# One batch's activations transposed by DMA instead of by TensorE, and a hand-written instruction order replaced

## The chip, the core and the metric

The kernel runs on one core of one Trainium2 chip. The metric is device time in microseconds (us) for one execution. Six engines matter: TensorE (PE in the profile; its weight loads, PEld, overlap the matmuls), VectorE (DVE), ScalarE (ACT), GpSimd (POOL), SyncE (SP, which issues DMAs), and the DMA engines, which are shared by all queues. In this kernel POOL issues all loads from DRAM except two, and SP issues the stores of the output and all DMA transposes. Each engine takes its instructions strictly in the order in which they were written; an instruction waits, on semaphores, for what it reads and for the buffers that it overwrites.

## What is computed

Causal attention with a window of 64 positions, followed by a two-layer network with the shrink function h - tanh(h):

```python
batch, n_heads, seq, head_dim = (8, 8, 576, 64)
n_tokens, d_model, d_ff = (4608, 512, 2048)

scores = scale * np.matmul(q, k.transpose(0, 1, 3, 2))
mask = (rel >= 0) & (rel < window)          # rel = query position - key position, window = 64
scores = np.where(mask, scores, -1000000000.0)
attn = softmax(scores)
attn_out = np.matmul(attn, v)
x = attn_out.transpose(0, 2, 1, 3).reshape(B * S, H * D)
h = x @ w_in
g = h - np.tanh(h)
return g @ w_out                            # 4608 x 512, float32
```

## The kernel before

**Attention.** A batch has 576 positions, that is nine windows of 64, and eight heads, taken as four pairs. Pair number g belongs to batch g // 4. For batches 0 to 2 q and k of a pair are loaded (steps `lk`, `lq`), cast to another layout (`ck`, `cq`), transposed by TensorE (`Fp` for k, `Ep` for q) and copied out of PSUM (`Fc`, `Ec`); `Rp` computes the scores of a pair in two groups, `Rx` the exponentials. From batch 3 on, q and k are loaded as token rows (`qr.b.i`, `lr.b.i`, five tiles of up to 128 tokens each) and transposed by DMA (`tq.b.i`, `tk.b.i`, on SP); `tz.b` copies the last 64 columns of q, `S.g` computes the scores of two pairs at once and `Sx` the exponentials. `M.g` masks (DVE). `PP.g` multiplies the probabilities of two pairs with v, with the sums in an extra column; `DR` and `DN` (DVE) divide and write x into the tile `xs`, two buffers, by batch modulo 2. v is loaded by `LV.b.i` (or `lv`, `lt` for batch 1) into `vw`, two buffers; since a window of keys straddles two row tiles, a copy across the partition halves follows: `Z.b` on DVE (lines 151 and 152), or `za`, `zb` for batch 1.

**The two layers.** The 4608 tokens are nine chunks of 512. x must stand with features on partitions. This is done for batches 0 to 3 by TensorE: `Xp.b.half.part.bank` transposes four or five windows (line 397) into a PSUM bank and `Xc` copies them into `xT`, the chunk tile. For batches 4 to 7 `Y.b.half` does it by DMA from `xs` on SP: a batch's nine windows lie in two chunks, so each `Y` issues two transposes. `H.c.m` is the first layer of chunk c for 128 of the 2048 hidden features (four matmuls of 512 columns, line 431); `Hp.c.m.half` is one half of it (line 508, two matmuls, those that need features half 0 or half 1 alone). `A` is tanh (ACT, line 439), `G` subtracts it (DVE, line 445). `W.c.s.part` is the second layer for 128 tokens and a quarter of the hidden features (four matmuls, line 474), and `O.c.s.engine` copies the finished PSUM bank to SBUF and issues its store from SP.

**The order.** The Tile framework runs with a manual schedule: no scheduler moves anything. A string, `PLAN`, lists some 1170 steps, and `play` calls them one after another; each appends its instructions to the queues of its engines. The order of the words in `PLAN` is thus the order of every engine's queue. A word's last letter, where there is one, names the engine: p POOL, a ACT, v DVE, s SP. PSUM has eight banks; two or three take turns for `H`, one or two for `W`, and the numbers in `Rp`, `Fp`, `Ep`, `Xp` name the others.

The steps that the diff and the prediction touch:

```python
    def x_dma(b, half):
        lo, hi = b * NJ, (b + 1) * NJ
        while lo < hi:
            c = lo // WPC
            to = min(hi, (c + 1) * WPC)
            nc.sync.dma_start(out=chunk_tile(c)[:, lo - c * WPC:to - c * WPC, half],
                              in_=xs[b % 2][:, half, lo - b * NJ:to - b * NJ].rearrange("p w r d -> p (w r d)"),
                              transpose=True)
            lo = to
```

Of the kernel before, what the change touches and what calls it, by code (L numbers as in the profile page):

```python
# [15 lines left out]
def kernel(  # L16
# [515 lines left out]
    def play(script):  # L532
# [21 lines left out]
        Rx.7.1.3 cq.9.v H.0.14 M.4 wo.3 zb.1.3.p G.0.12 Ec.8.1.a PP.4 wo.1 A.0.14 H.0.15 mk DR.4 DN.4.1 G.0.14  # L554
        A.0.15 H.0.13 DN.4.0 za.1.3.a W.0.0.0 Rp.8.0.3 G.0.15 A.0.13 Rp.8.1.5 DN.4.2 zb.1.2.a za.1.2.v Rx.8.1.5
        W.0.1.0 M.7 qr.3.3 LV.2.3 lk.11.p PP.6 Rx.8.0.3 Xp.1.0.1.3 W.0.0.2 G.0.13 Xp.1.0.0.4 DR.6 Xc.1.0.1.3.a
        DN.6.2 DN.6.0 W.0.1.2 DN.6.1 Xp.1.1.0.5 lk.10.p ck.9.a Xc.1.0.0.4.a Fp.9.3 Xc.1.1.0.5.a Xp.1.1.1.4
        lr.3.2 lq.10.p lq.11.p LV.2.2 Hp.1.0.0 Ep.9.7 Xc.1.1.1.4.v Ec.9.7.a Fc.9.3.a Hp.1.0.1 W.0.1.3 W.0.0.3
        qr.3.4 LV.2.0 Rp.9.1.5 Rp.9.0.3 LV.2.1 W.0.0.1 O.0.0.a M.8 LV.2.4 W.0.1.1 lr.3.1 lr.3.4 A.1.0 tq.3.4
        G.1.0 O.0.1.a Rx.9.1.5 Rx.9.0.3 ck.11.a M.9 ck.10.a W.0.2.1 W.0.2.0 W.0.2.3 W.0.2.2 W.0.3.2 qr.3.1  # L560
        O.0.2.a Fp.11.5 cq.10.v W.0.3.1 W.0.3.3 Hp.1.1.1 W.0.3.0 Fp.10.7 Ep.10.3 Hp.1.1.0 O.0.3.v Ec.10.3.v
        Hp.1.2.1 Hp.1.2.0 Fc.10.7.a A.1.1 A.1.2 Rp.10.1.3 G.1.1 cq.11.v G.1.2 Fc.11.5.a H.1.3 Ep.11.6 tk.3.2
        A.1.3 Rx.10.1.3 H.1.4 A.1.4 G.1.3 Ec.11.6.a H.1.5 A.1.5 qr.3.0 Z.2 H.1.6 qr.3.2 PP.8 G.1.5 Rp.11.0.3
        A.1.6 tk.3.1 tq.3.3 lr.3.0 H.1.8 Rx.11.0.3 G.1.4 G.1.6 DR.8 H.1.7 DN.8.2 A.1.8 A.1.7 H.1.9 tq.3.1 G.1.8
        H.1.11 G.1.7 A.1.9 tk.3.4 H.1.10 lr.3.3 A.1.11 A.1.10 DN.8.1 G.1.9 Rp.11.1.3 Rx.11.1.3 Rp.10.0.6 tq.3.2
# [12 lines left out]
        W.1.3.0 H.2.15 DN.14.2 O.1.3.a DN.14.1 A.2.15 A.2.14 DN.14.0 Xp.3.1.0.6 W.2.0.1 Xp.3.1.1.7 W.2.0.0
        G.2.14 W.2.0.2 Xc.3.1.1.7.v Xc.3.0.0.4.a Xc.3.1.0.6.a G.2.15 qr.5.0 Hp.3.0.0 W.2.0.3 Hp.3.1.1 Hp.3.1.0
        O.2.0.a A.3.1 W.2.1.1 Hp.3.0.1 W.2.1.2 G.3.1 tz.4.v A.3.0 S.16 Sx.16.2 W.2.1.3 Sx.16.1 G.3.0 H.3.3  # L580
        W.2.1.0 M.17 Sx.16.0 M.16 H.3.2 A.3.3 PP.16 G.3.3 O.2.1.a A.3.2 tk.5.2 qr.5.1 qr.6.4 H.3.5 LV.5.3
        W.2.2.1 DR.16 A.3.5 tk.5.1 DN.16.2 tq.5.2 G.3.2 DN.16.1 H.3.4 DN.16.0 Y.4.0 A.3.4 S.18 G.3.5 W.2.2.0
        H.3.7 G.3.4 Sx.18.1 A.3.7 Sx.18.2 G.3.7 W.2.2.3 H.3.6 A.3.6 Sx.18.0 tk.6.4 tk.5.3 tq.5.0 tq.5.1 H.3.9
        tk.5.0 M.19 W.2.2.2 G.3.6 qr.7.1 H.3.8 M.18 A.3.9 PP.18 A.3.8 O.2.2.v G.3.9 DR.18 G.3.8 DN.18.2 DN.18.1
        DN.18.0 W.2.3.0 W.2.3.3 H.3.11 qr.6.2 lr.6.0 LV.5.4 lr.6.2 LV.5.0 A.3.11 W.2.3.1 G.3.11 Y.4.1 tq.6.4
        H.3.10 W.2.3.2 A.3.10 tq.6.2 G.3.10 O.2.3.a H.3.13 H.3.14 A.3.13 LV.5.1 LV.5.2 lr.6.1 qr.6.1 A.3.14
        G.3.13 W.3.0.2 H.3.15 tz.5.v G.3.14 qr.6.3 H.3.12 W.3.0.0 A.3.15 G.3.15 Hp.4.1.0 A.3.12 G.3.12 Hp.4.1.1
        A.4.1 W.3.0.1 G.4.1 W.3.0.3 Hp.4.0.1 H.4.3 Hp.4.0.0 O.3.0.v tk.6.3 tk.6.2 A.4.0 S.20 A.4.3 Sx.20.2
        Sx.20.0 Sx.20.1 tq.6.0 tk.6.0 W.3.1.1 G.4.0 G.4.3 W.3.1.0 H.4.2 W.3.1.3 A.4.2 S.22 G.4.2 H.4.4 W.3.1.2
# [61 lines left out]
```

## Time and profile before

| | |
|---|---|
| runs | 307.33, 307.46, 308.23 us; median 307.46 |
| profiled execution | span 305.2 us, from the first to the last instruction |
| granted TensorE clock | full speed (1.00) in every 20 us stretch but the last (0.98) |
| TensorE busy | 297.8 us |
| DVE, ACT, POOL busy | 176.2, 157.5, 103.7 us |
| DMA | 36.77 MB in 132,878 packets, 119,920 of them under 512 bytes |

A row of the page's groups names line, engine, operation and tiles (out<-in), the number of instructions, then busy time and mean duration, then how long the engine was idle just before them and what ended that. A row of the timeline has start, duration of a merged group, engine and line, and in brackets the idle time before it with what ended it. The matmul pipeline overlaps: a matmul of 512 columns shows 380 ns, and starts every 216 ns behind another. Some matmul records are missing (2599 matmuls for 2632 weight loads), which leaves false idles of a fraction of a microsecond.

### The profile page before, as it was taken

What the parts mean: (1) busy time and instruction counts of PE and PEld (TensorE: products, weight loads), DVE (VectorE), ACT (ScalarE), POOL (GpSimd) and SP (SyncE); (2) the same over time, 40 slices, a digit from 0 to 9 for tenths busy, and PEclk for the clock granted to TensorE, in tenths of its full rate; (3) what the DMA queues carried; (4) which work ended last, traced back from release to release, by engine and by line L of the source; (5) the groups of instructions that cost most, each with busy time, mean ns of one, the idle gap of its engine ahead of it and who ended that gap; (6) DMA issues with size and microseconds to landing.
All of it is one profiled execution on the core that took longest, in us unless ns stands there. A gap on an engine that the chain in (4) does not pass through costs nothing.

```text
span 305.2 us, 6469 instructions
## 1 busy us (share of the span) xinstructions
PE 297.8 (98%) x2599; PEld 149.4 (49%) x2632; DVE 176.2 (58%) x316; ACT 157.5 (52%) x265; POOL 103.7 (34%) x141
## 2 busy tenths in 40 slices
PE   8999999999999999999999999999999999999995
PEld 3574555545455545444544444444544444444443
DVE  1687993289577745675387475657673645355300
ACT  1898975487565346534564645345633433433211
POOL 8989775800994290019005770000000000000000
PEclk9999999999999999999999999999999999999999
DMA  9999999995999999949999999560143010001112
GB/s 155 159 195 193 195 207 180 159 205 102 102 143 127 173 125 181 182 108 131 164 177 127 135 173 142 95 143 35 37 76 74 0 69 37 34 34 37 52 51 104
DMA packets 132878, 36.77 MB, mean 120 GB/s; under 512 B 119920, under 2 KB 127344, under 8 KB 132848
## 3 DMA queue, kind: packets, MB, share of 16 engines
q0 software_dynamic: 92752, 18.06, 85.3%
q1 hardware_dynamic: 40096, 18.30, 31.5%
q8 instruction: 20, 0.33, 0.5%
q14 instruction: 10, 0.08, 0.1%
HBM read 36.70 MB, written 9.44 MB: 151 GB/s over the span
## 4 chain that ended last, share of the span: by engine, by line
PE 87%; DVE 5%; ACT 3%; issue 2%; POOL 2%; DVEq 0%; ACTq 0%; POOLq 0%
PE ps L474 38%; PE ps L431 30%; PE ps L508 6%; PE ps L348 3%; PE ps L304 2%; DVE gT L445 2%; PE ps L397 1%; ACT th L439 1%; PE ps L286 1%; PE ps L467 1%; DVE pt L323 1%; PE ps L260 1%; PE ps L281 1%; PE ps L227 1%; POOL qall L110 1%
## 5 line engine op out<-in xcount | busy, mean ns | idle before, releaser
L445 DVE TENSOR_TENSOR gT<-ps,th 128x512 bf16<-128x512 f32 x144 | 97.2, 687 | 85.3 <-ACT th L439 84.6
L474 PE MATMUL ps<-w_out_sb,gT 128*128 128x512 bf16 x527 | 131.5, 380 | 2.2 <-issue 0.8
L439 ACT ACTIVATE th<-ps 128x512 f32<-128x512 f32 x144 | 84.7, 599 | 93.0 <-PE ps L431 79.7
L431 PE MATMUL ps<-xT,wi 128*128 128x512 bf16 x496 | 120.7, 380 | 0.1
L474 PEld LDWEIGHTS <-gT 128*128 128x128 bf16 x560 | 53.3, 98 | 61.4
L431 PEld LDWEIGHTS <-wi 128*128 128x128 bf16 x496 | 47.0, 98 | 54.3
L145 POOL DMA_DIRECT2D vw<-in_v_dram x35 | 30.0, 872 | 36.1 <-PE ps L348 33.5
L90 ACT ACTIVATE ysb<-ps 128x512 f32<-128x512 f32 (+1 forms) x24 | 14.2, 593 | 30.9 <-PE ps L474 30.2
L166 POOL DMA_DIRECT2D qall<-in_q_dram x25 | 21.7, 881 | 24.1 <-DMA qw<-qall 21.4
L166 POOL DMA_DIRECT2D kall<-in_k_dram x25 | 21.7, 875 | 10.4 <-DMA kw<-kall 4.8
L314 ACT ACTIVATE pt<-ps 128x1024 bf16<-128x1024 f32 (+1 forms) x30 | 23.3, 816 | 3.5 <-PE ps L304 3.2
L323 DVE TENSOR_TENSOR pt<-pt,ps 128x1152 bf16<-128x1152 bf16 x28 | 20.5, 749 | 5.1 <-ACT pt L314 3.2
L508 PE MATMUL ps<-xT,wi 128*128 128x512 bf16 x80 | 20.8, 380 | 0.0
L92 DVE COPY ysb<-ps 128x512 f32<-128x512 f32 (+1 forms) x11 | 7.1, 650 | 20.5 <-PE ps L467 13.2
L368 DVE TENSOR_TENSOR xs<-ps,rcp 128x384 bf16<-128x384 f32 x28 | 15.2, 550 | 0.3
L318 ACT ACTIVATE pt<-ps 128x640 bf16<-128x640 f32 (+1 forms) x24 | 14.7, 659 | 0.8 <-PE ps L286 0.8
L348 PEld LDWEIGHTS <-pt 128*64 128x64 bf16 x504 | 9.4, 112 | 6.3 <-DVE pt L323 2.1
L90 ACT ACTIVATE kt<-ps 128x576 bf16<-128x576 bf16 x10 | 6.5, 647 | 10.8 <-PE ps L256 6.8
L227 PE MATMUL ps<-warm 128*128 128x512 bf16 (+1 forms) x35 | 10.6, 435 | 1.1 <-DVE warm L207 1.1
L508 PEld LDWEIGHTS <-wi 128*128 128x128 bf16 x80 | 7.4, 98 | 8.5 <-issue 0.4
L348 PE MATMUL ps<-vw,pt 128*64 128x65 bf16 x504 | 11.0, 197 | 0.3 <-DVE pt L323 0.2
L365 DVE TENSOR_TENSOR xs<-ps,rcp 128x384 bf16<-128x384 f32 x14 | 7.7, 550 | 0.1
(74 smaller groups left out, 166.7 us busy)
## 6 DMA issues: line engine op xcount, KB each, us to landing
out_dram<-ysb SPq DMA_DIRECT2D x33, 256.0 KB, 3.1
vw<-in_v_dram POOLq DMA_DIRECT2D x28, 128.0 KB, 6.6
qall<-in_q_dram POOLq DMA_DIRECT2D x20, 128.0 KB, 7.5
kall<-in_k_dram POOLq DMA_DIRECT2D x20, 128.0 KB, 6.8
w_out_sb<-in_moe_w_out_dram POOLq DMA_DIRECT2D x4, 512.0 KB, 8.2
kall<-in_k_dram POOLq DMA_DIRECT2D x11, 144.0 KB, 6.3
qall<-in_q_dram POOLq DMA_DIRECT2D x11, 144.0 KB, 6.6
wi<-in_moe_w_in_dram POOLq DMA_DIRECT2D x3, 512.0 KB, 7.9
```

Source lines behind the costliest of these rows:

```text
L90: nc.scalar.activation(o, i, ACT.Copy)
L145: nc.gpsimd.dma_start(out=w[:, 2 * i + 1, :, 0:D] if i < NF else w[64:128, 2 * i, :, 0:D], in_=v[b, :, 128 * i:128 * i + n].rearrange("h p ...
L166: nc.gpsimd.dma_start(out=token_rows(b, n)[0:c, i], in_=(q if n == "q" else k)[b, :, 128 * i:128 * i + c].rearrange("h p d -> p h d"))
L314: nc.scalar.activation(o, sp, ACT.Exp, scale=scale)
L323: nc.vector.tensor_tensor(p, p, mask.unsqueeze(1).to_broadcast([128, 2 * NJ, 64]), ALU.mult)
L348: nc.tensor.matmul(ps[r, bank, 65 * i:65 * i + 65], PT[(g + r2) % NPT][:, j, r], vw[b % 2][:, j, p0 + r2 + NP * h, :], start=True, stop=True)
L368: nc.vector.tensor_tensor(xs[b % 2][:, p0 // 2, 0:6, n // 2, :], ov[:, :, 0:D], sums[g][:, n].to_broadcast([128, 6, D]), ALU.mult)
L431: nc.tensor.matmul(hp, w_in_tile(ki, m), chunk_tile(c)[:, n.start // 64:n.stop // 64, ki % 2, 64 * (ki // 2):64 * (ki // 2) + 64], start=( ...
L439: nc.scalar.activation(th[:, n], hp, ACT.Tanh)
L445: nc.vector.tensor_tensor(gT[c][:, m, columns(s)], hp, th, ALU.subtract)
L474: nc.tensor.matmul(yp, gT[c][:, m, s * 128:(s + 1) * 128], w_out_sb[:, m, :], start=n == 1 and i == 0, stop=n == 4 and i == 3)
L508: nc.tensor.matmul(hp, w_in_tile(half + 2 * i, m), chunk_tile(c)[:, :, half, 64 * i:64 * i + 64], start=n == 1 and i == 0, stop=n == 2 and ...
```

## The change

Only `PLAN` is changed; no function is. The first 230 words are the same in both, up to the masking step `M.4` in the last quarter of chunk 0's first layer. Behind it:

- `Xp.3.*` and `Xc.3.*` (18 transposes and four copies) are gone; `Y.3.0` and `Y.3.1` are new, each with two DMA transposes on SP.
- The casts of pairs 10 and 11 (`ck.10`, `ck.11`, `cq.10`, `cq.11`) go from ACT and DVE to POOL. Of batch 1's copies across halves `zb.1.3` goes from POOL to ACT, `za.1.3` from ACT to DVE and `zb.1.2` from ACT to DVE. `tz.4` goes from DVE to POOL, `tz.5` from DVE to ACT, and some twenty of the copies out of PSUM (`O`, `Xc`, `Fc`, `Ec`) change between ACT and DVE.
- Some of the banks of `Rp`, `Ep`, `Fp`, `Xp` of batches 1 and 2 are others.
- All other steps are the same ones in another order: loads, transposes on SP, both layers and the attention steps. `PP.24`, for instance, has 14 layer blocks' worth and a score block between the start of `PP.22` and itself (21 and one before), and the loads `LV.6.2`, `LV.6.0` and `lr.7.1` stand ahead of the loads that wait for `PP.22`.

```diff
-        Rx.7.1.3 cq.9.v H.0.14 M.4 wo.3 zb.1.3.p G.0.12 Ec.8.1.a PP.4 wo.1 A.0.14 H.0.15 mk DR.4 DN.4.1 G.0.14
-        A.0.15 H.0.13 DN.4.0 za.1.3.a W.0.0.0 Rp.8.0.3 G.0.15 A.0.13 Rp.8.1.5 DN.4.2 zb.1.2.a za.1.2.v Rx.8.1.5
...
-        Xp.3.0.1.3 A.2.8 G.2.8 tq.5.3 H.2.11 O.1.2.v PP.14 DR.14 H.2.10 A.2.11 A.2.10 Xc.3.0.1.3.v G.2.10
-        Xp.3.0.0.4 W.1.3.2 G.2.11 tq.5.4 W.1.3.3 H.2.12 A.2.12 H.2.13 Z.4 A.2.13 W.1.3.1 G.2.12 G.2.13 H.2.14
-        W.1.3.0 H.2.15 DN.14.2 O.1.3.a DN.14.1 A.2.15 A.2.14 DN.14.0 Xp.3.1.0.6 W.2.0.1 Xp.3.1.1.7 W.2.0.0
-        G.2.14 W.2.0.2 Xc.3.1.1.7.v Xc.3.0.0.4.a Xc.3.1.0.6.a G.2.15 qr.5.0 Hp.3.0.0 W.2.0.3 Hp.3.1.1 Hp.3.1.0
...
+        Rx.7.1.3 cq.9.v H.0.14 M.4 PP.4 wo.1 Ec.8.1.a G.0.12 Rp.8.1.3 A.0.14 wo.3 DR.4 DN.4.2 DN.4.0 G.0.14
+        DN.4.1 M.7 H.0.15 H.0.13 Ep.9.5 A.0.15 Rx.8.1.3 G.0.15 W.0.0.0 Xp.1.0.0.3 Rp.8.0.4 Xp.1.0.1.6 W.0.1.0
+        lk.10.p lk.11.p LV.2.0 lq.11.p LV.2.2 qr.3.1 lq.10.p lr.3.4 ck.11.p ck.10.p LV.2.3 cq.11.p LV.2.4 lr.3.3
+        lr.3.1 LV.2.1 lr.3.2 cq.10.p zb.1.3.a zb.1.2.v mk za.1.3.v Ec.9.5.a Rx.8.0.4 M.8 Xc.1.0.1.6.v za.1.2.v
...
+        W.0.2.0 W.0.2.3 W.0.3.1 Fc.9.3.a Rp.9.1.6 Rp.9.0.3 Rx.9.1.6 Rx.9.0.3 W.0.2.1 W.0.2.2 Ep.11.7 W.0.3.0
+        Fp.11.6 Fp.10.5 W.0.3.3 O.0.2.v M.9 G.1.0 Hp.1.1.1 Hp.1.1.0 Ec.11.7.a A.1.1 W.0.3.2 Fc.10.5.v G.1.1
+        Ep.10.5 H.1.3 Fc.11.6.a O.0.3.a A.1.3 Hp.1.2.1 Hp.1.2.0 Ec.10.5.a A.1.2 G.1.3 G.1.2 H.1.10 H.1.6
...
+        H.2.11 W.1.3.2 W.1.3.3 H.2.12 A.2.11 A.2.12 M.14 M.15 G.2.11 G.2.12 tk.4.0 tk.4.2 PP.14 W.1.3.0 H.2.14
+        W.1.3.1 A.2.14 DR.14 DN.14.0 DN.14.1 DN.14.2 LV.4.4 tz.4.p lr.6.2 G.2.14 H.2.13 Y.3.0 Y.3.1 qr.5.3
...
+        qr.6.4 qr.6.3 H.2.10 A.2.13 A.2.10 O.1.3.v G.2.13 W.2.0.1 H.2.15 G.2.10 S.16 W.2.0.0 A.2.15 G.2.15
+        Sx.16.0 Sx.16.2 M.16 Z.4 Sx.16.1 Hp.3.0.0 W.2.0.2 W.2.0.3 Hp.3.0.1 M.17 Hp.3.1.0 Hp.3.1.1 PP.16 A.3.0
...
+        W.3.3.0 H.4.12 H.4.11 tz.6.a A.4.12 G.4.12 W.3.3.2 H.4.10 A.4.11 A.4.10 G.4.11 G.4.10 W.3.3.3 H.4.13
+        S.24 LV.6.2 LV.6.0 lr.7.1 Y.5.0 Y.5.1 LV.7.4 LV.6.4 LV.6.3 lr.7.4 LV.6.1 qr.7.3 qr.7.0 LV.7.1 LV.7.2
+        qr.7.2 LV.7.0 tq.7.3 tq.7.1 tq.7.4 tq.7.0 lr.7.2 tk.7.1 tk.7.2 tq.7.2 O.3.3.v A.4.13 H.4.14 Sx.24.2
+        A.4.14 W.4.0.2 W.4.0.1 G.4.13 G.4.14 W.4.0.3 Hp.5.1.1 W.4.0.0 Sx.24.0 Sx.24.1 Z.6 M.24 M.25 Hp.5.1.0
+        A.5.1 O.4.0.a Hp.5.0.0 Hp.5.0.1 A.5.0 PP.24 W.4.1.0 W.4.1.2 G.5.1 DR.24 DN.24.1 DN.24.2 G.5.0 H.5.5
...
+        W.8.1.2 G.8.15 W.8.3.3 W.8.2.0 W.8.2.2 W.8.2.1 W.8.2.3 O.8.2.v W.8.3.2 W.8.1.3 O.9.0.v W.8.0.1 W.8.0.3
+        W.8.1.1 W.8.0.0 W.8.0.2 O.8.1.v O.8.0.a W.8.3.1 W.8.3.0 O.8.3.v"""
```

109 lines of the change are left out of this document (48 added, 61 removed).

## The prediction, made before the changed kernel was run

> **What bounds the kernel now.** I read the page's engine shares and chain first, then the windows view over the stretch that the diff touches (from block PP.4 to the last matmul), then the timelines of the engines around it. The page, and the one row of the windows view (length of the stretch, then busy time of PE, PEld, DVE, ACT, POOL):
>
> ```profile
> span 305.2 us, 6469 instructions
> PE 297.8 (98%) x2599; PEld 149.4 (49%) x2632; DVE 176.2 (58%) x316; ACT 157.5 (52%) x265; POOL 103.7 (34%) x141
> PE 87%; DVE 5%; ACT 3%; issue 2%; POOL 2%; DVEq 0%; ACTq 0%; POOLq 0%
> 38.69:301.90 263.21, 260.64 (x2105) 128.99 (x2138) 150.17 (x254) 128.28 (x217) 71.20 (x86) 1.00 1.14 112
> ```
>
> TensorE is the bound. In the 263.21 us concerned it is idle for 2.57 us, and part of that is only apparent: the page counts 2599 matmuls for 2632 weight loads, so 33 records are missing. Reordering alone can therefore win less than 2.57 us. What can win is less TensorE work; what can lose is any wait, because TensorE takes its blocks in the order of the list and nothing behind a late block overtakes it. DVE (150 of 263) and ACT (128) are a little over half busy.
>
> **The transposes taken out.** TensorE's timeline (start, duration of the merged group, instructions) has the four blocks of x of batch 3 among blocks of the two layers:
>
> ```profile
> 98.92 0.44 PE L397 MATMUL ps<-ident,xs 128*128 128x128 bf16 x5
> 99.20 1.03 PE L431 MATMUL ps<-xT,wi 128*128 128x512 bf16 x4
> ...
> 101.73 0.39 PE L397 MATMUL ps<-ident,xs 128*128 128x128 bf16 x4
> 101.95 1.89 PE L474 MATMUL ps<-w_out_sb,gT 128*128 128x512 bf16 x7
> ...
> 108.00 1.03 PE L431 MATMUL ps<-xT,wi 128*128 128x512 bf16 x4
> 108.86 0.39 PE L397 MATMUL ps<-ident,xs 128*128 128x128 bf16 x4
> 109.08 1.03 PE L474 MATMUL ps<-w_out_sb,gT 128*128 128x512 bf16 x4
> 109.95 0.44 PE L397 MATMUL ps<-ident,xs 128*128 128x128 bf16 x5
> 110.23 1.89 PE L474 MATMUL ps<-w_out_sb,gT 128*128 128x512 bf16 x7
> ```
>
> Matmuls overlap, so a block costs the distance to the next start, not its duration: 0.28 + 0.22 + 0.22 + 0.28 = **1.00 us** for 18 transposes. A layer block (H or W, four matmuls) costs 108.86 - 108.00 = 0.86. All other TensorE work is the same in both lists, block by block, and score, probability-value and full-array blocks change places 57 times in each, so the order adds no matmul time. The four PSUM copies that go with the transposes were on DVE and ACT, under TensorE's work: nothing.
>
> **Work moved between engines.** Four casts (two k, two q pairs of batch 2) go to POOL, three cross copies of v and about half of the output copies change between POOL, ACT and DVE. The copies lie under TensorE's blocks and have at least one block (0.86) of cover where a bank is reused, in both lists; if such a cover were short by 0.1 to 0.3 us it would cost that. Before's own wait of this kind, on TensorE's timeline:
>
> ```profile
> 90.14 0.47 PE L348 MATMUL ps<-vw,pt 128*64 128x65 bf16 x18
> 90.81 0.47 PE L348 MATMUL ps<-vw,pt 128*64 128x65 bf16 x18 [0.19 <-DVE pt L323]
> ```
>
> Such slips exist in the old list and will in the new; I let them cancel, with -0.5 (those of before vanish) to +0.5 as bounds.
>
> The casts stand in POOL's queue between loads, and each waits for its own load. No POOL cast of this shape (96x768) is in the trace. POOL's copy of v (view of tile vw, ns min/median/max) and its slowest row per element (groups by form, mean 293 ns), then the first and the last row of POOL's loads of that stage, and the time from issue to landing of its q load at 46.05:
>
> ```profile
> L92 POOL COPY vw<-vw x4: 612/614/642, 29.4 to 40.0; 64x520 bf16<-64x520 bf16 x4
> L231 POOL TENSOR_SCALAR_AFFINE_SELECT hide<-hide 128x128 bf16<-128x128 bf16 x1 | 0.3, 293 | 0.1
> 40.55 0.70 POOL L198 DMA_DIRECT2D w_out_sb<-in_moe_w_out_dram x1
> 58.73 1.80 POOL L166 DMA_DIRECT2D kall<-in_k_dram  x2 [0.34 <-issue]
> DMA to landing us min/median/max: 8.9/8.9/8.9
> ```
>
> By the copy's rate a cast is 614 x 768/520 = 0.9 us; by the slowest row it is 768 x 293/128 = 1.76. I take 0.9, since a cast is a copy. From 41.25 to 60.53 POOL issued 19 loads, 1.01 each with its waits. In the new list 14 loads and four casts stand before the last cast, cq.10: 41.25 + 14.1 + 3.6 = 59.0. Its user is Ep.10.5: from PP.4 (38.69) on stand 20 layer blocks' worth (17.2), two probability-value blocks (1.8), four score blocks, the transposes of x and five of q and k (about 3, at the rates of S below and of L397 above), so it is due near 60.7. 1.7 us of cover: **nothing**, with 0 and, at 1.76 a cast, 62.4, that is +1.7, as bounds. The loads of lq.11 and lq.10 are the fourth and seventh there; 8.9 us after an issue near 45 to 48 is before their casts.
>
> **x of batch 3 by DMA.** Two issues for each of Y.3.0 and Y.3.1, on SP, which waits most of the time. The time to landing depends on the loads beside them. Y.5.1's two issues (ns min/median/max, first and last start), the landing in us (min/median/max) of Y.4.1, of Y.5.0 and of Y.5.1, the loads that POOL begins 2 us ahead of Y.5.1, and on TensorE block PP.22, its next one, and a score block S:
>
> ```profile
> L416 SPq DMA_TRANSPOSE xT<-xs x2: 1180/1238/1295, 165.5 to 166.8; - x2
> DMA to landing us min/median/max: 4.9/6.0/7.1
> DMA to landing us min/median/max: 2.3/2.5/2.7
> DMA to landing us min/median/max: 7.6/7.9/8.2
> 163.41 4.18 POOL L145 DMA_DIRECT2D vw<-in_v_dram  x5 [18.06 <-PE ps L348]
> 162.51 0.77 PE L348 MATMUL ps<-vw,pt 128*64 128x65 bf16 x36
> 163.43 0.81 PE L474 MATMUL ps<-w_out_sb,gT 128*128 128x512 bf16 x3 [0.16 <-issue]
> ...
> 168.55 0.69 PE L304 MATMUL ps<-qw,kw 64*128 64x64 bf16 x34
> ```
>
> Without loads 2.5 us, with a burst that began 2 us ahead 7.6 to 8.2. Y.5.1's first issue, at 165.5, comes 3.0 us after its PP.22 starts at 162.51; Y.3.1 follows PP.14 in the same way. Its first half-chunk is used by Hp.3.0.1, behind PP.14 (0.92, from 162.51 to 163.43), a score block S (0.69 and its first two matmuls, 0.8) and 10.5 layer blocks: 0.92 + 0.8 + 9.0 = 10.7 us. POOL begins a burst there too, when tk.4.2 has landed. 3.0 + 4.9 to 3.0 + 7.6 is 7.9 to 10.6: just covered, so **nothing**; by the slowest row, 8.2, it is 0.5 late.
>
> **v of batch 6.** The tightest place I find is PP.24. It stands 14 layer blocks, a score block and PP.22 itself behind the start of PP.22: 12.0 + 0.8 + 0.92 = 13.7 us. Before PP.24, DVE must run Z.6 (the copies across partition halves, once LV.6.* has landed), M.24 and M.25. The masking M by the page's groups, Z alone on DVE, then Z beside POOL's loads; the landing of before's vw load at 165.8 and of the six vw loads from 163.4 on; and a stop of POOL in that burst:
>
> ```profile
> L323 DVE TENSOR_TENSOR pt<-pt,ps 128x1152 bf16<-128x1152 bf16 x28 | 20.5, 749 | 5.1 <-ACT pt L314 3.2
> 64.66 0.70 DVE L151 COPY vw<-vw 64x2080 bf16<-64x2080 bf16 x1
> 65.36 0.70 DVE L152 COPY vw<-vw 64x2080 bf16<-64x2080 bf16 x1
> ...
> 179.67 1.03 DVE L151 COPY vw<-vw 64x2080 bf16<-64x2080 bf16 x1
> 180.71 0.81 DVE L152 COPY vw<-vw 64x2080 bf16<-64x2080 bf16 x1
> DMA to landing us min/median/max: 8.1/8.1/8.1
> DMA to landing us min/median/max: 3.6/6.8/8.7
> 174.22 0.88 POOL L166 DMA_DIRECT2D qall<-in_q_dram  x1 [1.38 <-DMA xT<-xs]
> ```
>
> Z takes 1.4 to 1.85, and POOL is loading then, so 1.85. With M.24 (0.7) and the part of M.25 that the second half of PP.24 needs (0.35), LV.6.1 must have landed 13.7 - 2.9 = 10.8 us after PP.22's start. POOL's burst again begins 0.9 behind it, since LV.7.4 waits for PP.22, and LV.6.1 is fifth, behind three loads of 64 KB and one of 128, 448 KB with its own. The first landing row above is the one load that closed as many bytes in before's burst: issued at 165.8, landed at 173.9, 10.5 after the burst began. That gives 11.4: **0.5 us late** (0.6, less what DVE's pipelining takes off). Bounds: 0 if it lands by 10.8; the longest of that burst, 8.7 from an issue at +3.9, gives 12.6, 1.8 late. Behind Z.6, DVE's subtractions of chunk 5 wait too, but TensorE is then already standing at PP.24.
>
> On such copies beside POOL's loads the Trainium skill ("SBUF — State Buffer", Who interferes with whom) says that DVE copies in a two-port mode and POOL share one port pair as an exclusive lock, the loser waiting for the whole instruction. The four rows of Z agree that a copy suffers beside POOL (1.03 and 0.81 for 0.70). By that rule at its worst, a 0.9 us issue ahead of each copy, Z.6 takes 3.2 and the sum ends 1.35 us higher; the rows show a quarter of that.
>
> **The end.** The last output changes its mates: a store of 256 KB (O.8.0) is issued some 0.6 us before the last, of 64 KB. To landing, at the end:
>
> ```profile
> out_dram<-ysb SPq DMA_DIRECT2D x1, 192.0 KB, 1.9
> out_dram<-ysb SPq DMA_DIRECT2D x1, 64.0 KB, 1.6
> 301.60 1.03 SPq L485 DMA_DIRECT2D out_dram<-ysb  x2
> ```
>
> Before, 192 KB went 0.7 ahead of it. A quarter more bytes: **+0.1**, 0 to 0.4.
>
> **Sum.** The profiled execution spans 305.2, the runs' median is 307.46, 2.2 lie around the span in both. 307.46 - 1.00 + 0.5 + 0.1 = **307.06**, taken as 307.0. Its own range: 306.3 to 307.8.
>
> **Rivals.** *All in time.* LV.6.1 lands by 10.8 us and part of before's slips goes: 306.56 - 0.4 = 306.2. For it: the landing need be only 0.6 earlier, and three of the five loads are half size. Against it: Y.5.1 still runs through that burst. *x late.* Y.3.1 takes its 8.2 and its issue slips by one 1.2 us slot behind Y.3.0: Hp.3.0.1 stands 0.5 + 0.2 to 1.7, say 0.9, and with the 0.5 at PP.24 the time is 307.9. For it: a burst begins at the same moment. Against it: Y.4.1 had 4.9. *v later still (slower than before).* POOL can be stopped inside the burst until earlier DMAs are done, as by the 1.38 in the row at 174.22. If that falls ahead of LV.6.1 and it takes 8.7, it lands 3.9 + 1.4 + 8.7 = 14.0 us after PP.22, 3.2 late: 306.56 + 3.2 = 309.8; with half that stop, 309.1. It decides from a landing 12.7 us after PP.22, where the time passes 308.4. Against it: before's first stop in that burst came after eleven loads, not four. *Slow casts (slower).* At 1.76 each, and with lk.11 landing 8.9 us after an issue near 43, the first cast starts at 52; four casts (7.0) and the six loads between them (6.1) end at 65.1, 4.4 behind Ep.10.5's need: 311.5. Against it: the copy row.
>
> **How the numbers follow.** This kernel's measurement can tell about 0.3% (0.9 us) from no change: faster is below 306.54, slower above 308.38. Chances: forecast 0.42, all in time 0.28, x late 0.10, v later 0.14, slow casts 0.06. The first rival and a sixth of the forecast's range are faster: 0.35. The slower rivals with a few hundredths of forecast and x late: 0.25. The rest, 0.40, cannot be told from before. The range of 8 in 10 is 305.9 to 309.4: below, the first rival with 0.3 to spare; above, most of v later.
>
> **What would show it.** Right: L397 falls from 72 to 54, TensorE's busy time by 1.0 us or so, Hp.3.0.1 without an idle ahead of it, and at PP.24 an idle of about half a microsecond behind DVE's L151/L152 and a v load. Wrong: idle before the L508 block of chunk 3 behind a DMA into xT (x late), before L260 of pairs 10 or 11 behind a POOL copy (casts), or more than 1.9 us at PP.24. If TensorE's idle in the stretch behind PP.4 is 2 us above before's, some place that I gave full cover has none.

## The result

The changed kernel took 309.24 us (median of 20 runs, 307.31 to 312.88) against 307.77 for the kernel before (20 runs on the same chip, 307.02 to 309.03). The ratio is 1.0048, with a 95% interval of 1.0026 to 1.0069: **slower by 0.48%, some 1.5 us**, where a gain of 0.40 us, too small to tell from none, was forecast. The changed kernel's runs are also spread over 5.6 us, those of before over 2.0. Medians here and below are of all runs, while the ratios leave out single slow runs, over 1.5% above the fastest of their kernel (here the one at 312.88).

The profiled execution of the changed kernel took 308.1 us, less than the median. Its page (span, shares of the chain by engine, then two groups; the columns of a group are busy time and mean, then the idle time before and what ended it):

```profile
span 306.4 us, 6466 instructions
...
PE 59%; DMA 22%; POOL 10%; issue 4%; DVE 2%; SPq 1%; ACT 1%; POOLq 0%; DVEq 0%; ACTq 0%
...
L474 PE MATMUL ps<-w_out_sb,gT 128*128 128x512 bf16 x560 | 135.0, 379 | 1.4 <-ACT ysb L90 1.3
...
L166 POOL DMA_DIRECT2D qall<-in_q_dram x25 | 21.7, 878 | 23.0 <-DMA qw<-qall 22.2
```

Before, the chain that ended last was TensorE for 87%, and DMA did not appear in it at all. Now DMA has 22% of it and POOL 10%. And TensorE's second layer has an idle of 1.3 us that was ended by a copy on ACT into `ysb`, the buffer for the output. POOL's loads of q were held 22.2 us by a DMA transpose; this is not new, since the page of the kernel before has 21.4 us for it.

The stretch from block PP.4 to the last matmul (window, its length, then busy times of PE, PEld, DVE, ACT, POOL), to be read against the 263.21 of before:

```profile
39.25:303.19 263.94, 262.16 (x2121) 128.27 (x2120) 151.35 (x255) 122.04 (x206) 74.28 (x90) 1.00 1.17 114
```

It is 0.73 longer, although 1.00 of TensorE work is gone. TensorE's busy time says nothing here: 33 matmul records were missing before, and now the page counts 2614 matmuls for 2614 weight loads.

**Where it stands.** The changed kernel's TensorE timeline has one idle of more than half a microsecond behind PP.4, at W.3.3.1, the block ahead of PP.22:

```profile
163.66 1.02 PE L474 MATMUL ps<-w_out_sb,gT 128*128 128x512 bf16 x4 [1.34 <-ACT ysb L90]
164.61 0.57 PE L348 MATMUL ps<-vw,pt 128*64 128x65 bf16 x24
```

By starts of matmuls it is 1.50 us. So in this pair of executions the wait is the loss, within a quarter of a microsecond: 1.00 of work gone and 1.50 of waiting make +0.50, and the stretch is 0.73 longer. ACT's timeline names what the copy (step O.3.2) waited for, the store of an earlier output, since there are three `ysb` buffers:

```profile
163.01 0.60 ACT L90 ACTIVATE ysb<-ps 128x512 f32<-128x512 f32 x1 [4.69 <-DMA out_dram<-ysb]
```

The chain of waits goes on back from there (start, duration, what; lines in order of time):

```profile
133.08 2.44 DMA qw<-qall
...
136.05 0.83 POOL qall L166
...
137.79 7.04 DMA kall<-in_k_dram
...
145.11 9.77 DMA qall<-in_q_dram
...
154.90 1.57 SPq L179
...
157.85 5.06 DMA out_dram<-ysb
```

Read upwards: the copy waits for the store of O.2.3, issued at 157.85 and landed 5.06 later. The store stands on SP behind nine transposes of batch 6 (`tq.6`, `tk.6`); the eighth, tq.6.2, could not start before 154.90, when its load qr.6.2 had landed, 9.77 after its issue. That issue had itself waited on POOL, for 0.68, until lr.6.3, issued at 137.79, was there 7.04 later. Both belong to a burst of eleven loads that begins with qr.7.1 at 136.05, and qr.7.1 overwrites what the transpose tq.5.1 reads; this one is done at 133.08 + 2.44 = 135.52. The copy of O.2.3 itself, on DVE's timeline, was ready 19 us before its store was issued:

```profile
137.89 0.68 DVE L92 COPY ysb<-ps 128x512 f32<-128x512 f32 x1
```

SP's timeline, first of the changed kernel:

```profile
143.28 2.19 SPq L179 DMA_TRANSPOSE qw<-qall  x1
...
153.45 3.02 SPq L179 DMA_TRANSPOSE qw<-qall  x2
156.56 1.20 SPq L171 DMA_TRANSPOSE kw<-kall  x1
157.85 1.50 SPq L495 DMA_DIRECT2D out_dram<-ysb  x3
```

and of the kernel before, where three of batch 6's ten transposes stand ahead of O.2.3's store and not all ten (tk.6.4 further up, and the two in the first row), and it was issued 13.8 us earlier:

```profile
138.85 5.07 SPq L179 DMA_TRANSPOSE qw<-qall  x2
144.01 1.74 SPq L495 DMA_DIRECT2D out_dram<-ysb  x2
```

POOL's burst is no later than it was: in the kernel before it also begins with qr.7.1, which waits for tq.5.1 there too.

```profile
135.91 1.76 POOL L166 DMA_DIRECT2D qall<-in_q_dram  x2 [21.40 <-DMA qw<-qall]
```

What is new is the place of the store on SP.

### The profile page after: what moved, and what is told of

Same layout as the page of the kernel before. It is cut to its first block, busy times and chain, and to the rows that moved or that the text cites. A ratio compares the mean times of both kernels' runs of the same rounds, so it can differ in the third digit from the quotient of the medians.

```text
span 306.4 us, 6466 instructions
## 1 busy us (share of the span) xinstructions
PE 300.0 (98%) x2614; PEld 148.8 (49%) x2614; DVE 177.4 (58%) x317; ACT 151.1 (49%) x254; POOL 107.3 (35%) x145
## 4 chain that ended last, share of the span: by engine, by line
PE 59%; DMA 22%; POOL 10%; issue 4%; DVE 2%; SPq 1%; ACT 1%; POOLq 0%; DVEq 0%; ACTq 0%
PE ps L474 29%; PE ps L431 24%; DMA kall<-in_k_dram 6%; DMA qall<-in_q_dram 6%; DMA wi<-in_moe_w_in_dram 6%; DMA vw<-in_v_dram 3%; PE ps L508 2%; POOL vw L145 2%; PE ps L348 2%; POOL kall L110 2%; DMA out_dram<-ysb 2%; PE ps L304 1%; POOL qall L110 1%; PE ps L467 1%; POOL kall L166 1%
## 5 line engine op out<-in xcount | busy, mean ns | idle before, releaser
L474 PE MATMUL ps<-w_out_sb,gT 128*128 128x512 bf16 x560 | 135.0, 379 | 1.4 <-ACT ysb L90 1.3
L166 POOL DMA_DIRECT2D qall<-in_q_dram x25 | 21.7, 878 | 23.0 <-DMA qw<-qall 22.2
L166 POOL DMA_DIRECT2D kall<-in_k_dram x25 | 21.8, 887 | 12.3 <-DMA kw<-kall 10.2
L90 ACT ACTIVATE ysb<-ps 128x512 f32<-128x512 f32 x19 | 11.4, 599 | 24.7 <-PE ps L474 20.0
L92 DVE COPY ysb<-ps 128x512 f32<-128x512 f32 (+2 forms) x16 | 10.4, 652 | 20.1 <-PE ps L474 17.5
L368 DVE TENSOR_TENSOR xs<-ps,rcp 128x384 bf16<-128x384 f32 x28 | 14.9, 549 | 0.2
L227 PE MATMUL ps<-warm 128*128 128x512 bf16 (+1 forms) x35 | 11.4, 461 | 1.1 <-DVE warm L207 1.1
L90 ACT ACTIVATE kt<-ps 128x576 bf16<-128x576 bf16 x9 | 5.8, 649 | 7.6 <-PE ps L256 7.4
L110 POOL DMA_DIRECT2D kall<-in_k_dram x11 | 7.2, 658 | 2.7 <-DMA wi<-in_moe_w_in_dram 1.5
```

The source lines that it names most:

```text
L90: nc.scalar.activation(o, i, ACT.Copy)
L110: eng.dma_start(out=t, in_=(q if n == "q" else k)[b, pr::NP].rearrange("h (p e) d -> p h (e d)", e=E))
L166: nc.gpsimd.dma_start(out=token_rows(b, n)[0:c, i], in_=(q if n == "q" else k)[b, :, 128 * i:128 * i + c].rearrange("h p d -> p h d"))
L474: nc.tensor.matmul(yp, gT[c][:, m, s * 128:(s + 1) * 128], w_out_sb[:, m, :], start=n == 1 and i == 0, stop=n == 4 and i == 3)
```

## The experiments

Each kernel was timed in five rounds beside the kernel before (4 to 12 runs of each variant). The ratios are to it, with 95% intervals; what a variant gained against the changed kernel is the difference of two ratios, and so uncertain by about 0.3% (1 us). The changed kernel itself was not timed again beside the variants, which ran on four chips. In the expectations, e6_store_ahead is the kernel with nine transposes behind O.2.3, and e7 that with Y.4.1 ahead of tq.6.4 besides.

| kernel | median us | ratio | interval |
|---|---|---|---|
| changed | 309.24 | 1.0048 | 1.0026 to 1.0069 |
| changed, five `ysb` | 307.85 | 1.0006 | 0.9983 to 1.0029 |
| changed, two transposes behind O.3.2 | 308.30 | 1.0001 | 0.9983 to 1.0018 |
| before, five `ysb` | 307.51 | 0.9983 | 0.9965 to 1.0001 |
| before, x of batch 3 left out | 307.39 | 0.9994 | 0.9981 to 1.0007 |
| changed, nine transposes behind O.2.3 | 307.71 | 1.0004 | 0.9979 to 1.0028 |
| the same, and Y.4.1 ahead of tq.6.4 | 307.14 | 0.9970 | 0.9951 to 0.9990 |
| both of these, and five `ysb` | 307.14 | 0.9978 | 0.9959 to 0.9997 |
| changed, loads 4 us earlier | 314.80 | 1.0226 | 1.0204 to 1.0249 |
| changed, qr.7.1 last | 312.04 | 1.0130 | 1.0092 to 1.0167 |
| reordered stores and x, v ahead | 308.45 | 1.0011 | 0.9990 to 1.0032 |
| reordered stores and x, qr.7.1 last | 312.38 | 1.0140 | 1.0105 to 1.0174 |
| reordered stores and x, v moved up | 307.20 | 0.9971 | 0.9945 to 0.9997 |

### More output buffers in the changed kernel

```diff
+    y_pool = ctx.enter_context(tc.tile_pool(name="y", bufs=5))
...
-            ysb = sm_pool.tile([128, d_model], F32, tag="ysb", name="ysb")
+            ysb = y_pool.tile([128, d_model], F32, tag="ysb", name="ysb")
```

> The changed kernel with five buffers for the output copies instead of three; the order is untouched. Theory (stores): in the changed order the store of O.2.3 stands on SP behind the transposes tq.6.2 and tk.6.4, which wait for the last load of batch 6; with three buffers the copy O.3.2 then waits for that store and TensorE stands at W.3.3.1 (1.50 us in the profile of the changed kernel, 161.94 on). Five buffers take that wait away: 1.5 to 2.5 us less than the changed kernel, about 307.0, and the spread of its runs (307.3 to 312.9) shrinks to about that of before (2 us). Rival (late v or x): the time is lost at PP.24 or at the first layer of a chunk, and the wait at W.3.3.1 only hides it: within 0.5 us of the changed kernel's 309.2, with an idle at one of those places. Rival (casts on POOL): unchanged, 309.2.

307.85, 1.0006: 1.4 us less than the changed kernel by the medians. Its runs still spread over 3.7 us, and not over the 2 expected. Its TensorE timeline has no idle at W.3.3.1 (last row), but one at H.4.3, where the changed kernel had none (the line numbers of this kernel are one higher):

```profile
143.83 0.82 PE L432 MATMUL ps<-xT,wi 128*128 128x512 bf16 x3 [1.69 <-DMA xT<-xs]
...
163.35 1.03 PE L475 MATMUL ps<-w_out_sb,gT 128*128 128x512 bf16 x4
```

So the buffers take this wait away, the medians fall by about what it shows, with an uncertainty of 1 us, and a second place is late in some executions: H.4.3 waits for Y.4.1, the DMA transposes of x of batch 4, which stand on SP behind tq.6.4.

### Two transposes moved behind the copy that waited

```diff
-        tq.6.3 tq.6.2 tk.6.4 W.2.3.3 H.3.10 H.3.15 S.20 A.3.10 O.2.3.v
+        tq.6.3 W.2.3.3 H.3.10 H.3.15 S.20 A.3.10 O.2.3.v
...
-        DN.20.2 O.3.2.a H.4.8
+        DN.20.2 O.3.2.a tq.6.2 tk.6.4 H.4.8
```

> The changed kernel with two steps moved on SP alone: tq.6.2 and tk.6.4 go behind O.3.2, so that the stores of O.2.3, O.3.0 and O.3.1 no longer wait for the last loads of batch 6. Theory (stores): the same gain as with five buffers, about 307.0 us, and no idle at W.3.3.1; S.24, which needs tq.6.2 and tk.6.4, stands 9 us behind and is not late. Rival (the late loads themselves): S.24 becomes the place of the wait and the time stays near 309. Rival (casts on POOL): unchanged, 309.2.

308.30, 1.0001. The median fell by 0.9, but the profile does not show the reason expected. SP's store and then TensorE:

```profile
156.39 1.51 SPq L495 DMA_DIRECT2D out_dram<-ysb  x3
```

```profile
163.86 1.02 PE L474 MATMUL ps<-w_out_sb,gT 128*128 128x512 bf16 x4 [1.27 <-ACT ysb L90]
```

The store went only 1.5 us earlier, since tq.6.3, still ahead of it, was late too, and TensorE waited as before. Not two transposes but the whole block of nine is in the way. The ratio is as low as with five buffers although the wait is in this profile, so the fall of a median cannot be put down to this one wait with certainty.

### More output buffers in the kernel before

The same edit as the first, in the kernel before.

> The kernel before with five buffers for the output copies. Theory (stores): its order has no such wait, so the same time as before, 307.8 us within 0.4. Rival (three buffers hold up any order, or their place in memory matters): 0.5 us or more faster than before.

307.51, 0.9983, with an interval that holds 1. The buffers are no gain in the old order: the wait belongs to the new one.

### The kernel before without the transposes of x of batch 3

All `Xp.3.*` and `Xc.3.*` are left out, nothing takes their place, and so this part of x is not computed.

```diff
-        Xp.3.0.1.3 A.2.8 G.2.8 tq.5.3 H.2.11 O.1.2.v PP.14 DR.14 H.2.10 A.2.11 A.2.10 Xc.3.0.1.3.v G.2.10
-        Xp.3.0.0.4 W.1.3.2 G.2.11
+        A.2.8 G.2.8 tq.5.3 H.2.11 O.1.2.v PP.14 DR.14 H.2.10 A.2.11 A.2.10 G.2.10
+        W.1.3.2 G.2.11
...
```

> The kernel before without the 18 transposes of x of batch 3 on TensorE and without their four copies, and with nothing in their place: that part of x is left out. This measures what the change takes from TensorE. By the starts in the trace of before, 1.00 us: 306.8. Rival (the transposes fill time in which TensorE would wait anyway): 307.8, no difference.

307.39, 0.9994: at most 0.6 us faster by the interval, not 1.0. TensorE's timeline:

```profile
115.88 0.56 PE L304 MATMUL ps<-qw,kw 64*128 64x64 bf16 x26 [0.39 <-DMA qw<-qall]
```

TensorE now comes 1.2 us earlier to the score block S.16 (115.05 instead of 116.27), but the q that it reads is transposed by a DMA whose time is set by loads. By starts of matmuls the new wait is 0.56 us, so a good half of the gain is lost there. In this execution of the old order the transposes filled time that TensorE would partly have spent waiting.

### The nine transposes moved behind O.2.3's store

```diff
-        G.3.13 LV.5.0 qr.6.2 tq.6.4 Y.4.1 tq.6.0 tk.6.3 tk.6.0 tk.6.2 tq.6.1 tk.6.1
-        tq.6.3 tq.6.2 tk.6.4 W.2.3.3 H.3.10 H.3.15 S.20 A.3.10 O.2.3.v
+        G.3.13 LV.5.0 qr.6.2 tq.6.4 Y.4.1 W.2.3.3 H.3.10 H.3.15 S.20 A.3.10 O.2.3.v
+        tq.6.0 tk.6.3 tk.6.0 tk.6.2 tq.6.1 tk.6.1 tq.6.3 tq.6.2 tk.6.4
```

> The changed kernel with the nine transposes tq.6.* and tk.6.* moved behind O.2.3 in the order of SP; nothing else is moved. O.2.3's store then leaves at about 139 us instead of 157. Theory (stores): the idle at W.3.3.1 (1.4 to 1.5 us in two profiles) is gone, and the time is that of five buffers, 307.8; what then still varies is H.4.3, which waits for the x of batch 4 (Y.4.1) in some executions. Rival (SP and its loads are late as a whole): the wait moves to S.24 or stays at W.3.3.1, and the time stays above 308.7.

307.71, 1.0004, as with the five buffers and by another way. The profiled execution took 310.02, more than the median; it has no idle at W.3.3.1 (the last row), but two others of more than 0.9 us:

```profile
145.14 0.82 PE L431 MATMUL ps<-xT,wi 128*128 128x512 bf16 x3 [2.12 <-DMA xT<-xs]
...
158.02 0.76 PE L348 MATMUL ps<-vw,pt 128*64 128x65 bf16 x36 [0.91 <-DVE vw L152]
...
165.63 1.03 PE L474 MATMUL ps<-w_out_sb,gT 128*128 128x512 bf16 x4
```

The first is H.4.3 again. The second is PP.20: `Z.5`, the copies of v of batch 5 across the halves (L151 and L152), is late because the load LV.5.0 is the tenth of POOL's burst.

### Y.4.1 ahead of tq.6.4 as well

```diff
-        LV.5.0 qr.6.2 tq.6.4 Y.4.1 W.2.3.3
+        LV.5.0 qr.6.2 Y.4.1 tq.6.4 W.2.3.3
```

> As e6_store_ahead, and Y.4.1 before tq.6.4 on SP, so that x of batch 4 is issued 1.2 us earlier and ahead of the loads that tq.5.1 sets free. Theory (the late x is the second place): Y.4.1 lands before H.4.3 in nearly all executions, 0.5 to 1 us less than e6_store_ahead, 307.0, and the spread of the runs is that of before, 2 us. Rival (the loads beside it set its landing, not its issue): as e6_store_ahead, 307.8, with an idle inside H.4.3 where there is one.

307.14, 0.9970 (0.9951 to 0.9990): **faster than both kernels**. H.4.3 no longer waits in the profile; PP.20 still does, and DVE's timeline shows for what:

```profile
155.07 0.76 PE L348 MATMUL ps<-vw,pt 128*64 128x65 bf16 x36 [1.24 <-DVE vw L152]
```

```profile
153.61 0.70 DVE L151 COPY vw<-vw 64x2080 bf16<-64x2080 bf16 x1 [1.33 <-DMA vw<-in_v_dram]
```

### The same with five output buffers

The kernel of 307.14, with the five output buffers of the first experiment.

> e7_store_and_x_ahead with five buffers for the output copies. If these two places are all that the new order lost, the buffers add nothing: within 0.3 us of e7, 307.0. Rival (other output copies wait for buffers too): 0.5 us or more less than e7.

307.14, 0.9978. With the store in time, more buffers add nothing, as it must be if buffers and the store's place cure the same wait.

### The burst of loads started earlier

The chain begins with tq.5.1, for which POOL's burst waits. Here it is moved up on SP, ahead of tk.5.3, tk.5.4, tk.5.0 and Y.4.0.

```diff
-        tq.5.2 tk.5.1 lr.5.0
+        tq.5.2 tk.5.1 tq.5.1 lr.5.0
...
-        tk.5.0 Y.4.0 tq.5.1 O.2.2.v
+        tk.5.0 Y.4.0 O.2.2.v
```

> The changed kernel with one transpose, tq.5.1, moved on SP from behind Y.4.0 to behind tk.5.1. POOL's load qr.7.1, which overwrites its source, and the ten loads behind it then start near 128 us instead of 136. Theory (POOL's standstill, from 119 to 136, is what makes the batch-6 transposes and so the store late): tk.6.4 and O.2.3's store are issued 6 us or more earlier and W.3.3.1 has no idle, with the store still behind the transposes; x of batch 4 then meets the burst and may be up to 2 us late at H.4.3: 307.0 to 308.7. Rival (the loads run at the rate of the DMA engines whenever they start, or SP's own waits keep the store late): 309.2 as the changed kernel.

314.80, 1.0226: neither theory nor rival. The loads do start earlier, at 131.67 instead of 136.05, but Y.4.0 and Y.4.1 now run beside them, and O.2.3's store is no earlier (158.13). Landing of the four DMAs into `xT` (min/median/max, us; 2.4/2.6/5.3 in the changed kernel), then TensorE and its windows (length, busy times, then the granted clock as the third number from the right):

```profile
DMA to landing us min/median/max: 6.2/8.0/9.1
```

```profile
148.82 1.46 PE L431 MATMUL ps<-xT,wi 128*128 128x512 bf16 x3 [4.84 <-DMA xT<-xs]
```

```profile
143.60:148.80 5.20, 0.38 (x2) 0.00 (x0) 0.95 (x2) 0.00 (x0) 1.21 (x2) 0.98 1.94 110
148.80:151.50 2.70, 2.68 (x7) 1.03 (x8) 0.55 (x1) 1.18 (x2) 0.00 (x0) 0.50 1.67 156
```

TensorE stands 4.84 us at H.4.3, and the seven matmuls after it run at half the clock. It also waits 1.71 us at W.1.1, at 84.53, which lies ahead of the edit.

### The load that holds POOL moved to the end of the burst

POOL does nothing for 17 us because qr.7.1 waits. Here it goes behind the ten other loads of the burst (the expectation says eleven).

```diff
-        A.3.11 A.3.8 G.3.8 qr.7.1 qr.6.0
+        A.3.11 A.3.8 G.3.8 qr.6.0
...
-        G.3.13 LV.5.0 qr.6.2 tq.6.4 Y.4.1
+        G.3.13 LV.5.0 qr.6.2 qr.7.1 tq.6.4 Y.4.1
```

> The changed kernel, with one load of batch 7 (qr.7.1, which waits for the transpose tq.5.1 and holds POOL idle from 119 to 136 us) moved behind the eleven loads that stand after it. SP's order is left as it is, with tq.6.2 and tk.6.4 ahead of the store of O.2.3. Theory (the late store at W.3.3.1 is late because qr.6.2 is, and qr.6.2 is late because qr.7.1 stands ahead of it): qr.6.2 lands before 140 instead of at 154.9, O.2.3's store is issued by about 140 and lands by 150, W.3.3.1 has no idle (1.50 goes), and v of batch 5 lands early too, so that PP.20 isn't late: 306.9, between 306.2 and 307.6. Rival (the loads just collide elsewhere: the eleven loads now run from 119 on beside tk.5.* and Y.4.0, whose landings lengthen as Y.4.1's did to 9.1 us when loads were moved earlier): 309 or more, with an idle of 1 us or more at S.20, H.4.3 or PP.18.

312.04, 1.0130: the rival held. The transposes `tk.5.*` from issue to landing (min/median/max), first in the changed kernel, then here:

```profile
DMA to landing us min/median/max: 2.5/4.2/4.5
```

```profile
DMA to landing us min/median/max: 7.4/8.3/8.9
```

and TensorE here:

```profile
133.56 0.81 PE L474 MATMUL ps<-w_out_sb,gT 128*128 128x512 bf16 x2 [1.56 <-DVE ysb L92]
...
142.93 0.62 PE L304 MATMUL ps<-qw,kw 64*128 64x64 bf16 x30 [2.08 <-DMA qw<-qall]
```

The loads of v and of batch 6 are early now, and the transposes and stores of batch 5 are late instead: a store ahead of W.2.3.2 and q of S.20. Three stores that SP issues from 125 on, the one ahead of W.2.3.2 among them, land in 7.5 to 8.3 us; in the changed kernel they took 4.6 to 4.8.

### Only v moved into POOL's idle time; qr.7.1 last with the other two edits

The first of two kernels built on the one that took 307.14 moves the loads of v of batch 5 ahead of qr.7.1, the second moves qr.7.1 as above.

```diff
-        A.3.11 A.3.8 G.3.8 qr.7.1 qr.6.0
-        tz.5.a lr.6.3 lr.6.1 LV.5.1 qr.7.4 LV.5.2 LV.5.3 lr.6.4
+        A.3.11 A.3.8 G.3.8 LV.5.1 LV.5.2 LV.5.3 LV.5.0 qr.7.1 qr.6.0
+        tz.5.a lr.6.3 lr.6.1 qr.7.4 lr.6.4
...
-        G.3.14 G.3.13 LV.5.0 qr.6.2 Y.4.1
+        G.3.14 G.3.13 qr.6.2 Y.4.1
```

> The kernel with the batch 6 transposes behind O.2.3's store and Y.4.1 ahead of tq.6.4 (307.14), and besides the four loads of v of batch 5 (LV.5.0 to LV.5.3) moved ahead of qr.7.1, that is into POOL's idle time from 119 on. Theory (what is left of the loss is PP.20, 1.4 late in that kernel's profile because Z.5 waits for LV.5.0 behind qr.7.1): LV.5.0 lands before 135, no idle at PP.20, and the time is 306.2, between 305.7 and 306.8. Rival (PP.20's wait only moves to the next late place, as S.16's did when the transposes were taken from the kernel before): 307.0 to 307.4. Second rival (four loads of v beside tk.5.* and Y.4.0 make these late): 308 or more.

> The kernel with the batch 6 transposes behind O.2.3's store and Y.4.1 ahead of tq.6.4 (307.14), and besides qr.7.1 moved behind the eleven loads after it, so that POOL doesn't stand from 119 to 136. Theory (one blocking load is the root of the three late places W.3.3.1, H.4.3 and PP.20): the time is 306.2, between 305.7 and 306.8, and not below the kernel with qr.7.1 alone moved by more than 0.7, since with the loads early SP's order hardly matters. Rival (the loads run beside tk.5.* and Y.4.0 and make them late): 308 or more.

308.45 (1.0011) and 312.38 (1.0140). By the ratios, four loads in POOL's idle time cost 1.3 us against the kernel of 307.14 and ten cost 5.2, each uncertain by about 1. In the first, PP.20 is no longer late, but TensorE waits at two other places:

```profile
113.67 1.45 PE L508 MATMUL ps<-xT,wi 128*128 128x512 bf16 x6 [0.98 <-DMA xT<-xs]
...
134.34 1.89 PE L474 MATMUL ps<-w_out_sb,gT 128*128 128x512 bf16 x7 [2.13 <-DVE ysb L92]
```

The second row is W.2.3.2, as in the experiment with qr.7.1 last. The first is Hp.3.0.1, waiting for x of batch 3: this place lies ahead of the edit and the list up to it is that of the changed kernel, where it did not wait. The other kernel waits at W.1.1, again ahead of the edit; there the output copy stands on DVE behind Z.3, which DVE began after 1.86 us of idle:

```profile
83.81 1.46 PE L474 MATMUL ps<-w_out_sb,gT 128*128 128x512 bf16 x6 [1.45 <-DVE ysb L92]
```

### v moved up inside the burst

On the kernel that took 307.14; qr.7.1 stays first and the burst starts when it did.

```diff
-        tz.5.a lr.6.3 lr.6.1 LV.5.1 qr.7.4 LV.5.2 LV.5.3 lr.6.4 DN.18.0
+        tz.5.a lr.6.3 LV.5.1 LV.5.2 LV.5.3 LV.5.0 lr.6.1 lr.6.4 DN.18.0
...
-        G.3.14 G.3.13 LV.5.0 qr.6.2 Y.4.1
+        G.3.14 G.3.13 qr.6.2 qr.7.4 Y.4.1
```

> The kernel with the batch 6 transposes behind O.2.3's store and Y.4.1 ahead of tq.6.4 (307.14), and besides the four loads of v of batch 5 moved up inside POOL's burst that starts at 136: they stay behind qr.7.1, which holds the burst back, but go ahead of lr.6.1, lr.6.4, qr.7.4. So nothing is loaded earlier than 136, and the landings of tk.5.*, Y.4.0, tq.5.1 and Y.4.1 stay as they are. Theory (PP.20 is 1.4 late there because LV.5.0 is the tenth load of the burst; as the seventh it lands near 150.6 instead of 153.6): no idle at PP.20, and the time is 306.2, between 305.7 and 306.8. Rival (the wait only moves on to the next late place behind PP.20, W.3.3.1 or PP.22, as part of the transposes' gain did at S.16): 306.9 to 307.4.

307.20, 0.9971: no gain in the median. The profile has the step as the theory had it, PP.20 without idle, and the stretch from PP.4 to the last matmul:

```profile
154.92 0.76 PE L348 MATMUL ps<-vw,pt 128*64 128x65 bf16 x36
```

```profile
39.90:302.04 262.14, 259.61 (x2088) 128.11 (x2120) 151.83 (x255) 122.07 (x206) 73.31 (x88) 1.00 1.13 114
```

262.14 is 1.07 less than before's 263.21, the gain of the transposes, whole; neither execution has a wait of more than 0.2 in this stretch. So the median is the rival's, but the profile doesn't show the rival's wait at a later place. And PP.4 begins at 39.90 in this execution and began at 38.69 in before's, although TensorE's list up to there is the same, and so the two take nearly the same time. Whether PP.20 was late in this kernel's other runs, or how often it is in the 307.14 kernel's, one profile each cannot tell.

## Why the prediction failed

The forecast was a change of -0.40 (307.46 to 307.06); measured were +1.5. By its steps:

**The copies and their cover: the step that failed.** The prediction said that the output copies "lie under TensorE's blocks and have at least one block (0.86) of cover where a bank is reused", priced reordering at nothing, within 0.5, and said of SP that it "waits most of the time". It looked at the engine that makes the copy and at the PSUM bank, not at the buffer that the copy writes. That buffer comes free by a store, the store stands in SP's order, and in the new order it stands behind nine transposes that wait for loads. The price, put at nothing, is 1.50 us in the profile; taken away in two ways, by two more buffers or by the store's place, the ratio falls from 1.0048 to 1.0006 and 1.0004, some 1.3 us, uncertain by 1. The fall alone doesn't single this wait out, since it was as large for the kernel with two transposes moved, which still waited; that the wait is new, and what it hangs on, is in the profiles. An SP that waits most of the time is not free time for what stands behind the wait.

**The same mistake, smaller.** Y.4.1 behind tq.6.4 (ahead of it in the old order) and the last load of v of batch 5 as the tenth of POOL's burst (the eighth in the old order) are two further changes of order that the prediction did not price. The first, mended, takes the ratio from 1.0004 to 0.9970, about 1 us with an uncertainty as large; the profile of the changed kernel did not wait there, those of two variants did (1.69 and 2.12). Both places on SP mended, the ratio falls from 1.0048 to 0.9970, some 2.4 us and clear of the noise; how much of it belongs to which is not. For the second, 1.33 of DVE's waiting was seen, and no gain was measured by mending it.

**The transposes.** 1.00 us for 18 is right as TensorE's time: the 54 left, and the stretch of the last experiment, 1.07 shorter. It is a gain only where the next load-bound block has slack: in one execution of the old order 0.56 of it was lost at S.16. The sign that the prediction named, a fall of TensorE's busy time by 1.0, could not show: the busy time rose, from 260.64 to 262.16, with the records that before's trace lacks, and for the same reason the idle fell from 2.57 to 1.78 where a rise by 2 was to give a late place away.

**PP.24: forecast 0.5 late, measured 0.** DVE's `Z.6` by the view of tile vw, what it waited for, and TensorE's blocks there:

```profile
L151 DVE COPY vw<-vw x1: 842/842/842, 175.3 to 175.3; 64x2080 bf16<-64x2080 bf16 x1
L152 DVE COPY vw<-vw x1: 968/968/968, 176.2 to 176.2; 64x2080 bf16<-64x2080 bf16 x1
...
  DMA vw<-in_v_dram: 0.8, 1
```

```profile
176.91 1.46 PE L508 MATMUL ps<-xT,wi 128*128 128x512 bf16 x6
178.30 0.82 PE L348 MATMUL ps<-vw,pt 128*64 128x65 bf16 x36
```

The two copies took 1.81, as costed (1.85). Z.6 did wait for v, but the load was there 10.6 us after PP.22's start (164.61 to 175.2) and not 11.4; the need was 10.8. The mechanism was right, the landing 0.8 too long.

**The casts: right.** Four on POOL, by groups of the changed kernel, 0.83 to 0.85 each against 0.9 in the sum, and the transposes that need them never waited (last two rows, idle 0.0):

```profile
L92 POOL COPY qb<-qall 96x768 bf16<-96x768 bf16 x2 | 1.7, 850 | 0.0
L92 POOL COPY kb<-kall 96x768 bf16<-96x768 bf16 x2 | 1.6, 825 | 0.4 <-DMA kall<-in_k_dram 0.4
```

```profile
L260 PE MATMUL ps<-ident,qb 96*128 96x96 bf16 x54 | 3.8, 206 | 0.0
L260 PE MATMUL ps<-ident,kb 96*128 96x96 bf16 x54 | 3.5, 206 | 0.0
```

**x of batch 3 by DMA: right in the profile of the changed kernel, but not safe.** Its TensorE timeline runs through Hp.3.0.1 without idle:

```profile
111.63 1.89 PE L474 MATMUL ps<-w_out_sb,gT 128*128 128x512 bf16 x8
113.36 1.46 PE L508 MATMUL ps<-xT,wi 128*128 128x512 bf16 x6
```

In one variant, with the same list up to there, it waited 0.98: the rival "x late" comes true in some executions.

**The end.** From the last matmul to the end of the span it is 3.2 us (306.4 less 303.19) and was 3.3: nothing, for the 0.1 forecast.

**The sum again.** -1.00 and nothing else would be -0.33%; the reordered kernels stand at 0.9970 and 0.9971. Forecast and measurement differ by 1.9 us: about 1.3 for the store, about 1 for Y.4.1, less the 0.5 that PP.24 did not cost; the first two are uncertain by 1 us each, so that their sum fits is no proof. The measured 309.24 lies inside the range of 305.9 to 309.4, but by luck: its upper part was there for v of batch 6 at PP.24, which cost nothing. **What stays open:** the profiled run of the changed kernel, with its one wait, took 308.1, and half of its runs took over 309.2. What those lost is in no profile of it. Three of the 20 runs (310.55, 311.24 and 312.88) have a mean granted clock of 0.994, as have the profiled executions of the kernels with the loads earlier and with qr.7.1 last, in which TensorE ran at half its clock behind a stall; so these three probably had such a stall, while others of up to 311.3 ran at 1.00. The waits that the variants show at places with the same order (H.4.3, PP.20, Hp.3.0.1, W.1.1; 0.5 to 2.1 each) are what it may be, and that was not shown for the changed kernel itself.

## What to carry to other kernels

When a step moves in a hand-written order, follow the buffer that it writes to the end: what frees it, in which queue that stands, and what the entry ahead of it there waits for; a copy hidden under TensorE can hang on a load three queues away. Idle time of a loading engine is not free capacity where transposes and stores share the DMA engines: beside 17 us of POOL's idleness the transposes of batch 5 landed in 2.5 to 4.5 us, with its loads moved there in 7.4 to 8.9, and such moves cost 1.3 to 5.2. Where margins are about as large as the spread of landings, one profile shows which places can be late and only the medians show what they cost.

## What the runs showed of the hardware

The same DMA transposes land in 2.5 to 4.5 us, or in 7.4 to 8.9, by what POOL loads beside them (`tk.5.*`, above).

TensorE ran at half its clock for about 3 us after a stall: behind the 4.84 us at H.4.3, seven matmuls at a granted clock of 0.50. In the kernel with qr.7.1 last it followed an idle of only 2.08, up to 142.93; the window behind it in that kernel:

```profile
142.90:147.60 4.70, 4.45 (x41) 2.08 (x42) 1.95 (x3) 2.28 (x4) 3.51 (x4) 0.66 1.62 162
```

The Trainium skill ("TensorE: Matmul & The Clock Gate", Part 1) describes a clock that halves after an idle window of about 3.4 us. The first case agrees; the second shows that a shorter stall was enough, where only a few short matmuls stood beside it (from 140.40 to 142.93 TensorE was busy for 0.45 of 2.53 us). Here a wait of 2 us cost some 1.6 us more, an estimate from 4.70 us at 0.66 instead of 1.00.
